# Constants of an attention and mixture-of-experts kernel: from GpSimd's DMA queue to ScalarE's, two of them as rows that TensorE turns into columns

## The chip, the cores and the metric

The kernel runs on one core of a Trainium2 chip. The metric is the device time of one execution in microseconds. Three runs of the kernel before gave 579.92, 584.13 and 584.41 us, a median of 584.13 us.

## The reference: what is computed

Two stages, all in fp32 for the reader of the output:

```python
# q, k, v: [8 batches, 8 heads, 576 tokens, 64]; g_norm: [64]
kv  = einsum('bhsd,bhse->bhde', k, v)          # 64 x 64 for each head
out = einsum('bhsd,bhde->bhse', q, kv)
x   = out / sqrt(mean(out*out, -1) + 1e-6) * g_norm   # -> [4608 tokens, 512]
# mixture of experts, top 1: w_gate [512, 8], w1 [8, 512, 1024], w2 [8, 1024, 512]
logits = x @ w_gate;  e = argmax(logits);  gate = softmax(logits)[e]
# the first `capacity` tokens of each expert are kept, the others give zero
out[i] = gate * relu(x[i] @ w1[e]) @ w2[e]
```

The small inputs are `g_norm` (64 floats), `w_gate` (512 x 8 floats) and `capacity` (one 64-bit integer, here 1152). They are the constants of which the change speaks.

## The kernel before

**Attention** goes through the eight batches in order. A batch's k, v and q come in two halves of four heads each; a half is loaded by two DMAs of SyncE's (SP's) queue (lines 685 and 686: 512 KB in rows of 1 KB, and 64 KB in rows of 256 bytes), in the order k, v, k, v, q, q. Three buffers stand ready for each of k, v and q. TensorE (PE) makes kv of each pair of heads (line 707), ScalarE or VectorE copies it out as `kvs` and into a block-diagonal table `kv_bd`, PE turns `kvs` (line 731) and multiplies it by the gate weights `wgs` (line 740), so that the logits of a token come out of the same product as its row: `kv_bd` has 64 + 8 columns for each head. PE turns q (line 771) and multiplies it by `kv_bd` (line 789). VectorE, ScalarE and GpSimd (POOL) work out the norm, the expert and the place of each token, and POOL writes the rows to a scratch tensor `x_dram` (lines 1006 and 1008).

**Experts** follow one after the other: weights are loaded by SP's queue, split into fp16 high and low parts, the expert's rows are gathered by indirect DMAs, and PE makes both products (lines 522 and 568) from three fp16 terms each. The result is scattered by indirect DMAs (line 598).

**Where the constants are used.** `g_norm` stands as a column `gcol`, one value for each of 128 partitions (the 64 values twice). It scales the gate weights once (line 265, in place) and later the scale of the first expert matrix (lines 347 and 366). `cap` is the capacity as a column and is used when the tables of the tokens that are left over are made, hundreds of us later. `wgs` is first read by PE at line 740, in the first batch.

**What sets the order.** Everything ahead of the planner (memsets, iotas, the loads of the constants, line 265) is put into the engines' streams by the framework's scheduler. From the first load of k on, the class `Plan` lists operations with their engine, estimated duration, key and what they need, places them greedily, and the instructions are then emitted in that order, engine by engine (`manual_schedule`). Each engine runs its stream strictly in order. DMAs of the hardware queues (SP's and ScalarE's) count on eight completion semaphores, taken in turn (`DMAHW0` to `DMAHW7` in the listings below); a DMA whose semaphore is still in use waits on its issuing engine until the earlier DMA on that semaphore has landed. DMAs of POOL's queue have eight of their own (`DMASW0` to `DMASW7`).

Of the kernel before, what the change touches and what calls it, by code (L numbers as in the profile page):

```python
# [11 lines left out]
F32 = mybir.dt.float32  # L12
I32 = mybir.dt.int32
AF = mybir.ActivationFunctionType
ALU = mybir.AluOpType
# [29 lines left out]
FIRST = -50.0  # L45
# [33 lines left out]
class Ring:  # L79
# [3 lines left out]
    def new(self):  # L83
        self.holds.append(Hold(self.holds[-self.n] if len(self.holds) >= self.n else None))
        return self.holds[-1]
# [8 lines left out]
class Plan:  # L94
# [5 lines left out]
    def op(self, ways, fn, deps=(), key=0.0, takes=(), uses=(), late=0.0):  # L100

        ways = [ways] if isinstance(ways[0], str) else list(ways)
        o = Op(ways, fn, [d for d in deps if d is not None], list(takes), key, late)
        for h in takes + uses if isinstance(takes, tuple) and isinstance(uses, tuple) else list(takes) + list(uses):
            h.users.append(o)
        self.ops.append(o)
        return o
# [56 lines left out]
def attention_moe_kernel(  # L164
# [12 lines left out]
    nc = tc.nc  # L177
    NB, H, S, D = q.shape
# [3 lines left out]
    P = 128  # L182
# [10 lines left out]
    cst = ctx.enter_context(tc.tile_pool(name="cst", bufs=1))  # L193
# [10 lines left out]
    ones = cst.tile([1, P], F32, name="ones")  # L204
# [43 lines left out]
    warm = cst.tile([1, 1], F32, name="warm")  # L248
    nc.vector.memset(warm, 0.0)
    nc.scalar.activation(warm, warm, AF.Exp)  # L250
    cap_i = cst.tile([P, 2], I32, name="cap_i")
    nc.gpsimd.dma_start(cap_i, capacity.bitcast(I32).rearrange("(o x) -> o x", o=1).broadcast_to([P, 2]))
    cap = cst.tile([P, 1], F32, name="cap")
    nc.vector.tensor_copy(cap, cap_i[:, 0:1])

    gcol = cst.tile([P, 1], F32, name="gcol")
    for h2 in range(2):
        nc.gpsimd.dma_start(gcol[h2 * D:(h2 + 1) * D], g_norm.rearrange("(d o) -> d o", o=1))

    wgs = cst.tile([P, 2, 2, 2, E], F32, name="wgs")  # L260
    nc.vector.memset(wgs, 0.0)
    for f in range(2):
        for i in range(2):
            nc.gpsimd.dma_start(wgs[i * D:(i + 1) * D, f, i], w_gate.rearrange("(f i g p) e -> f i p g e", f=2, i=2, g=2)[f, i])
    nc.vector.tensor_scalar(out=wgs, in0=wgs, scalar1=gcol, scalar2=None, op0=ALU.mult)


    kv_bds = []
# [377 lines left out]
    tab, misc = bank("tab"), bank("misc")  # L646
# [17 lines left out]
    op = plan.op  # L664
# [5 lines left out]
    def copy(e, out_, in_):  # L670
        if e == "A":
            nc.scalar.copy(out_, in_)  # L672
        else:
            nc.vector.tensor_copy(out_, in_)

    issued, waits = [], []

    def load(b):
        ts = {}
        for j, (nm, half) in enumerate(ORDER):  # L680
            h = new(nm)
            h.t, h.flat = ios[nm, (len(rings[nm].holds) - 1) % NIO]

            def go(e, h=h, src={"k": k, "v": v, "q": q}[nm], hs=slice(half * HH, (half + 1) * HH)):
                nc.sync.dma_start(h.t[:, :, 1:C], src[b, hs, HP:S].rearrange("h (p c) d -> p h c d", c=C - 1))
                nc.sync.dma_start(h.t[0:HP, :, 0], src[b, hs, 0:HP].rearrange("h p d -> p h d"))

            o = op(("S", ISSUE), go, [], (b - 2) * C + j * 0.8, takes=(h,))
            ts[nm, half] = h, op(("D", LOAD), None, [o], takes=(), uses=(h,))
            issued.append(o)  # L690
        return ts

    def kv_products(b, ts):

        key = (b - 1) * C + 1
        kv = new("kv")
        kv2 = kv.t = kv_bds[b % 2]
        a = new("a")
        rows = [slice(0, D), slice(D, P)]

        def product(i):
            def go(e):
                a.t = a.t or bank("a")
                for c in range(C):
                    for g in range(2):
                        h = 2 * (i % 2) + g
                        nc.tensor.matmul(a.t[rows[g], i * D:(i + 1) * D], lhsT=kh.t[:, h, c, :], rhs=vh.t[:, h, c, :],
                                         start=(c == 0), stop=(c == C - 1))

            kh, vh = ts["k", i // 2][0], ts["v", i // 2][0]  # L710
            return op(("T", 1.16), go, [ts["k", i // 2][1], ts["v", i // 2][1]], key, (a,), (kh, vh))

        mm = [product(i) for i in range(HH)]
        ks, kt, a2, a3 = new("kvs"), new("kvt"), new("a"), new("a")

        def apart(e):
            ks.t = at.tile([P, HH * D], F32, name="kvs", bufs=1)
            copy(e, ks.t, a.t[:, 0:HH * D])

        done = [op([("A", 0.29), ("V", 0.34)], apart, mm, key + 1, (ks,), (a,))]  # L720

        def spread(g, f):

            return op([("A", 0.29), ("V", 0.34)],
                      lambda e: copy(e, kv2[rows[f]].rearrange("p (i g) f x -> p i g f x", g=2)[:, :, g, f, 0:D],
                                     ks.t[rows[g]].rearrange("p (i x) -> p i x", i=HH)), done[0:1], key + 1.5, (kv,), (ks,))

        def turn(e):
            a2.t = bank("a")
            for f in range(2):  # L730
                nc.tensor.transpose(a2.t[:, f * P:(f + 1) * P], ks.t[:, f * P:(f + 1) * P], ident)

        def keep(e):
            kt.t = at.tile([P, 2 * P], F32, name="kvt", bufs=1)
            copy(e, kt.t, a2.t[:, 0:2 * P])

        def gates(e):
            a3.t = bank("a")
            for f in range(2):
                nc.tensor.matmul(a3.t[:, f * 4 * E:(f + 1) * 4 * E], lhsT=kt.t[:, f * P:(f + 1) * P],  # L740
                                 rhs=wgs[:, f].rearrange("p i g e -> p (i g e)"), start=True, stop=True)

        o = op(("T", 0.22), turn, done[0:1], key + 1, (a2,), (ks,))
        o = op([("A", 0.29), ("V", 0.34)], keep, [o], key + 1, (kt,), (a2,))
        o = op(("T", 0.2), gates, [o], key + 1, (a3,), (kt,))
        done = [spread(g, f) for g in range(2) for f in range(2)]
        for g in range(2):
            for f in range(2):
                done.append(op([("A", 0.11), ("V", 0.13)],
                               lambda e, g=g, f=f: copy(  # L750
                                   e, kv2[rows[f]].rearrange("p (i g) f x -> p i g f x", g=2)[:, :, g, f, D:XW],
                                   a3.t[rows[g], 0:H * E].rearrange("p (i g x) -> p i g x", g=2, x=E)[:, :, g]),
                               [o] + done[4:], key + 2, (kv,), (a3,)))
        return kv, done
# [493 lines left out]
    def finish():  # L1248
# [8 lines left out]
        early["rank"] = op(("V", 3.4), lambda e: rank_experts(cnt_all), [o, o2], key + 0.1)  # L1257

    tiles = {0: load(0)}
    kvs = {0: kv_products(0, tiles[0])}  # L1260
    for b in range(NB):
        oh, ssh = new("o"), new("ss")
        oh.t, ssh.t = o_sbs[b % NO], sss[b % NO]
        if b + 1 < NB:
            tiles[b + 1] = load(b + 1)
        outs, sums, by_u = [], [], {}
        for n in range(len(UNITS)):
            done = unit(b, n, tiles[b], *kvs[b], oh)
            outs += done
            u = UNITS[n][1]  # L1270
            by_u.setdefault(u, []).extend(done)
            if UNITS[n][0]:
                sums += [squares(b, c, by_u[u], oh, ssh) for c in range(2 * u, min(2 * u + 2, C))]
            if n == 1 and b + 1 < NB:
                kvs[b + 1] = kv_products(b + 1, tiles[b + 1])
        route(b, oh, ssh, outs, sums)
        if b == PICK_AFTER:
            early_weights()
        if b == EARLY_AFTER:
            early_slots()  # L1280
# [210 lines left out]
    op = plan.op  # L1491
# [8 lines left out]
    def weights(r, key, after, after2):  # L1500

        ws, sets, zs, holds = wsets[r % 2], [], [], []
        for i in range(2):
# [9 lines left out]
            for p in range(4):  # L1513
                o = op(("S", 0.7), lambda e, i=i, p=p, regs=regs: load(e, i, p, regs),
                       [regs.get("op"), early["rank"]] + after + (early["free"][p] if r == 1 and i == 0 else [])
                       + (after2 if i else []), key,
                       (raws[p],))
                regs.setdefault("op", o)
                loads.append(op(("D", 1.46), None, [o], key, (), (raws[p],)))
# [115 lines left out]
    o = op(("S", 0.01), moved, [early["scaled"]], -9 * KEY, (), tuple(ews))  # L1635
# [6 lines left out]
    for r in range(E):  # L1642
        products(r, *args)
        key = KEY * r
        if r + 1 < E:
            before = [] if r > 1 else sent
            st, xs_hold, sl, gates, turned, sent, asked = rows_beside(r + 1, key + ROWS)
# [3 lines left out]
        else:  # L1651
            steps, o = plan_rest(), early["later"]
            for _ in range(68):
                o = op(("V", 0.2), lambda e: next(steps, None), [o], key + 1)
# [36 lines left out]
```

## Time and profile before

| what | us |
|---|---|
| runs: lowest, median, highest | 579.92, 584.13, 584.41 |
| the profiled execution | 582.53 |
| its span | 580.7 |
| PE busy | 530.1 (91%) |
| VectorE (DVE) busy | 384.1 (66%) |
| ScalarE (ACT) busy | 256.0 (44%) |
| GpSimd (POOL) busy | 218.2 (38%) |

The span is the time between the first and the last instruction of the program's record; 1.8 us of the profiled execution lie outside it. Busy times are sums over stages with different limits, so the stage that holds the change has to be read by itself. SPq is SP's queue, in which DMAs are issued; the time of such an instruction is the time of its issue, not of the transfer.

### The profile page before, as it was taken

Reading aid. Unit: us, or ns where it says so; the run is one execution under the profiler, and the core shown is the slowest. Engines: PE = TensorE matmul, PEld = TensorE weight load, DVE = VectorE, ACT = ScalarE, POOL = GpSimd, SP = SyncE. Lnnn points to the kernel's source line nnn. Section 1 sums busy time; section 2 is a strip of 40 time slices with the busy share of each in tenths; the row PEclk is TensorE's granted clock in tenths of the full one; section 3 lists DMA queues with packets and bytes.
Section 4 is the critical chain, followed back from the end, with each engine's and each line's share of the span. In section 5 each row is a group of like instructions: output and inputs, shape, how many; then the busy total and the mean of one; then the engine's idle time right before and its main releaser. Section 6 shows DMA issues by size and latency. Waiting matters only on the chain.

```text
span 580.7 us, 11581 instructions
## 1 busy us (share of the span) xinstructions
PE 530.1 (91%) x4339; PEld 354.9 (61%) x4339; DVE 384.1 (66%) x998; ACT 256.0 (44%) x498; POOL 218.2 (38%) x300
## 2 busy tenths in 40 slices
PE   1887999777887999998999999999999999999995
PEld 1886998666543656643765477477558747845442
DVE  2386687989985898999999375738638634731200
ACT  1465675678621356372725252453525355211210
POOL 7002053265315478384342713364163352011011
PEclk9999899999999999999999999999999999999999
DMA  7999999956228759697864653847265342001001
GB/s 208 291 301 332 326 309 345 333 174 247 93 92 306 204 113 358 122 309 206 217 227 118 169 174 98 209 102 240 82 171 181 110 82 68 1 36 40 1 20 48
DMA packets 94302, 102.56 MB, mean 177 GB/s; under 512 B 51314, under 2 KB 75890, under 8 KB 93216
## 3 DMA queue, kind: packets, MB, share of 16 engines
q1 hardware_dynamic: 86240, 70.43, 44.6%
q0 software_dynamic: 8000, 31.32, 15.4%
q8 instruction: 36, 0.59, 0.4%
q14 instruction: 26, 0.21, 0.1%
HBM read 73.13 MB, written 20.61 MB: 161 GB/s over the span
## 4 chain that ended last, share of the span: by engine, by line
PE 28%; issue 19%; DMA 12%; DVE 11%; POOL 6%; ACT 2%; POOLq 0%; DVEq 0%; SPq 0%
PE hp L522 12%; PE yp L568 12%; DMA out_dram<-ysb,si 8%; DVE w2l L377 3%; DMA xg<-x_dram,gi 2%; DVE am L337 2%; POOL xg L433 2%; DVE hl L530 2%; PE yp L577 1%; POOL pair L469 1%; POOL xm L441 1%; PE op L522 1%; DMA raw<-in_moe_w_dram 1%; POOL out_dram L598 1%; DVE w1l L377 1%
## 5 line engine op out<-in xcount | busy, mean ns | idle before, releaser
L522 PE MATMUL hp<-xs,w1h 128*128 128x320 f16 (+6 forms) x896 | 133.5, 300 | 1.8 <-DVE hl L530 1.7
L522 PEld LDWEIGHTS <-w1h 128*128 128x128 f16 x960 | 93.2, 98 | 42.5 <-issue 5.6
L568 PEld LDWEIGHTS <-hh 128*128 128x128 f16 x560 | 54.4, 98 | 64.6 <-issue 1.9
L598 POOL DMA_INDIRECT out_dram<-ysb,si x41 | 42.2, 1030 | 135.3 <-ACT ysb L593 104.1
L527 ACT ACTIVATE hh<-hp 128x320 f16<-128x320 f32 (+7 forms) x64 | 40.7, 636 | 110.5 <-PE hp L522 110.4
L337 DVE TENSOR_REDUCE am<-raw 128x1 f32<-128x512 f32 x120 | 75.4, 674 | 6.5 <-DMA raw<-in_moe_w_dram 6.3
L522 PE MATMUL hp<-xs,w1l 128*128 128x320 f16 (+6 forms) x448 | 71.5, 300 | 0.0
L530 DVE SCALAR_TENSOR_TENSOR hl<-hp,hh 128x320 f16<-128x320 f32 (+7 forms) x64 | 47.2, 737 | 34.0 <-ACT hh L527 33.6
L469 POOL TENSOR_TENSOR pair<-xm,pair 128x512 f16<-128x512 f32 (+5 forms) x35 | 43.0, 1228 | 69.0 <-ACT pair L465 64.1
L568 PE MATMUL yp<-w2h,hl 128*128 128x512 f16 x272 | 66.0, 385 | 0.0
L789 PE MATMUL op<-kv_bd,qt 128*128 128x144 f32 (+1 forms) x384 | 57.9, 293 | 8.1 <-ACT qt L672 3.2
L568 PE MATMUL yp<-w2h,hh 128*128 128x512 f16 x272 | 64.6, 379 | 0.8 <-ACT ysb L593 0.8
L568 PE MATMUL yp<-w2l,hh 128*128 128x512 f16 x272 | 64.5, 379 | 0.0
L593 ACT ACTIVATE ysb<-yp,ysc 128x512 f32<-128x512 f32 (+5 forms) x40 | 27.3, 683 | 81.7 <-PE yp L568 68.7
L377 DVE SCALAR_TENSOR_TENSOR w2l<-raw,sw,w2h 128x512 f16<-128x512 f32 x64 | 53.2, 878 | 9.5 <-ACT w2h L371 9.5
L433 POOL DMA_INDIRECT xg<-x_dram,gi x41 | 42.7, 1040 | 42.1 <-DVE gi L632 29.2
L522 PEld LDWEIGHTS <-w1l 128*128 128x128 f16 x480 | 46.7, 98 | 19.0
L789 PEld LDWEIGHTS op<-kv_bd,qt 128*128 128x128 f32 x384 | 50.1, 195 | 11.8 <-ACT o_sb L672 4.6
L377 DVE SCALAR_TENSOR_TENSOR w1l<-raw,sg,w1h 128x512 f16<-128x512 f32 x64 | 52.3, 868 | 1.7 <-ACT w1h L371 1.7
L568 PEld LDWEIGHTS <-hl 128*128 128x128 f16 x280 | 27.3, 99 | 33.2 <-issue 2.2
L371 ACT ACTIVATE w1h<-raw,sg 128x512 f16<-128x512 f32 x62 | 39.8, 712 | 7.3 <-DVE sg L366 7.2
L371 ACT ACTIVATE w2h<-raw,sw 128x512 f16<-128x512 f32 x62 | 39.7, 710 | 3.0 <-PE yp L577 2.1
(249 smaller groups left out, 651.7 us busy)
## 6 DMA issues: line engine op xcount, KB each, us to landing
raw<-in_moe_w_dram SPq DMA_DIRECT2D x64, 512.0 KB, 5.1
x_dram<-o_sb POOLq DMA_DIRECT2D x8, 1152.0 KB, 8.1
k_sb<-in_k_dram SPq DMA_DIRECT2D x16, 512.0 KB, 7.5
v_sb<-in_v_dram SPq DMA_DIRECT2D x16, 512.0 KB, 7.4
q_sb<-in_q_dram SPq DMA_DIRECT2D x16, 512.0 KB, 8.4
x_dram<-o_sb POOLq DMA_DIRECT2D x8, 144.0 KB, 7.9
k_sb<-in_k_dram SPq DMA_DIRECT2D x16, 64.0 KB, 7.1
v_sb<-in_v_dram SPq DMA_DIRECT2D x16, 64.0 KB, 7.9
```

The costliest lines, as they stand in the source:

```text
L337: nc.vector.tensor_reduce(out=am()[:, p:p + 1], in_=raw[:, sl(p)], axis=AX.X, op=ALU.max, apply_absolute_value=True)
L371: nc.scalar.activation(wh[:, sl(p)], raw[:, sl(p)], AF.Copy, scale=z["s"])
L377: nc.vector.scalar_tensor_tensor(out=wl[:, sl(p)], in0=raw[:, sl(p)], scalar=z["s"], in1=wh[:, sl(p)], op0=ALU.mult, op1=ALU.subtract)
L433: nc.gpsimd.indirect_dma_start(out=self.xg[i][0:n], out_offset=None, in_=x_dram[0:self.rows, :], in_offset=bass.IndirectOffsetOnAxis(ap=se ...
L469: nc.gpsimd.tensor_tensor(out=pair[0:n, 1], in0=self.xm[i][0:n], in1=pair[0:n, 0], op=ALU.subtract)
L522: nc.tensor.matmul(self.view(hp)[:, u], lhsT=w[:, c, j * P:(j + 1) * P], rhs=x[:, c, u * hw:(u + 1) * hw], start=(t == 0 and c == 0), stop ...
L527: nc.scalar.activation(self.out(self.hh, j), self.view(hp), AF.Relu)
L530: nc.vector.scalar_tensor_tensor(out=self.out(self.hl, j), in0=self.view(hp), scalar=0.0, in1=self.out(self.hh, j), op0=ALU.max, op1=ALU.s ...
L568: nc.tensor.matmul(yp[0:n, 0:DM], lhsT=h[:, j, o:o + n], rhs=w[:, j, :], start=(m == 0), stop=(m == len(self.terms) - 1))
L593: nc.scalar.activation(self.ysb[0:n], yp[0:n, 0:DM], AF.Copy, scale=self.ysc[0:n, i:i + 1])
L598: nc.gpsimd.indirect_dma_start(out=out[:, :], out_offset=bass.IndirectOffsetOnAxis(ap=self.sidx[0:n, col:col + 1], axis=0), in_=ysb[0:n], ...
L789: nc.tensor.matmul(ph.t[:, j * m:(j + 1) * m], lhsT=qt.t[:, i * P:(i + 1) * P], rhs=x, start=True, stop=True)
```

## The change

The six small loads leave POOL's queue for ScalarE's. `w_gate` still comes as before, four DMAs of 64 partitions. `g_norm` now comes once, as a row of 64 values in one partition, and `capacity` as two integers in one partition. Three new operations of the plan make columns of them: VectorE doubles the row and casts the capacity (`widen`), PE multiplies the row by a one and the capacity by a row of ones, into two columns of a PSUM bank (`constants`), VectorE copies the two columns out and scales `wgs` (`columns`). PE's product with `wgs` names `columns` as something that it needs. POOL issues no DMA before `x_dram`'s first.

```diff
-    cap_i = cst.tile([P, 2], I32, name="cap_i")
-    nc.gpsimd.dma_start(cap_i, capacity.bitcast(I32).rearrange("(o x) -> o x", o=1).broadcast_to([P, 2]))
+    cap_i = cst.tile([1, 2], I32, name="cap_i")
     cap = cst.tile([P, 1], F32, name="cap")
-    nc.vector.tensor_copy(cap, cap_i[:, 0:1])
+    caprow = cst.tile([1, 1], F32, name="caprow")
 
     gcol = cst.tile([P, 1], F32, name="gcol")
-    for h2 in range(2):
-        nc.gpsimd.dma_start(gcol[h2 * D:(h2 + 1) * D], g_norm.rearrange("(d o) -> d o", o=1))
+    grow = cst.tile([1, 2, D], F32, name="grow")
+    one = cst.tile([1, 1], F32, name="one")
+    nc.vector.memset(one, 1.0)
 
     wgs = cst.tile([P, 2, 2, 2, E], F32, name="wgs")
     nc.vector.memset(wgs, 0.0)
     for f in range(2):
         for i in range(2):
-            nc.gpsimd.dma_start(wgs[i * D:(i + 1) * D, f, i], w_gate.rearrange("(f i g p) e -> f i p g e", f=2, i=2, g=2)[f, i])
-    nc.vector.tensor_scalar(out=wgs, in0=wgs, scalar1=gcol, scalar2=None, op0=ALU.mult)
+            nc.scalar.dma_start(wgs[i * D:(i + 1) * D, f, i], w_gate.rearrange("(f i g p) e -> f i p g e", f=2, i=2, g=2)[f, i])
+    nc.scalar.dma_start(grow[:, 0], g_norm.rearrange("(o d) -> o d", o=1))
+    nc.scalar.dma_start(cap_i, capacity.bitcast(I32).rearrange("(o x) -> o x", o=1))
...
+    def constants(e):
+        nc.tensor.matmul(misc[:, 128:129], lhsT=grow.rearrange("o h d -> o (h d)"), rhs=one, start=True, stop=True)
+        nc.tensor.matmul(misc[:, 129:130], lhsT=ones, rhs=caprow, start=True, stop=True)
+
+    def columns(e):
+        nc.vector.tensor_copy(gcol, misc[:, 128:129])
+        nc.vector.tensor_copy(cap, misc[:, 129:130])
+        nc.vector.tensor_scalar(out=wgs, in0=wgs, scalar1=gcol, scalar2=None, op0=ALU.mult)
+
+    def widen(e):
+        nc.vector.tensor_copy(grow[:, 1], grow[:, 0])
+        nc.vector.tensor_copy(caprow, cap_i[:, 0:1])
+
+    ready = op(("V", 0.2), widen, [], FIRST, late=9.0)
+    ready = op(("V", 0.5), columns, [op(("T", 0.2), constants, [ready], FIRST)], FIRST)
...
-        o = op(("T", 0.2), gates, [o], key + 1, (a3,), (kt,))
+        o = op(("T", 0.2), gates, [o, ready], key + 1, (a3,), (kt,))
```

The order of the streams moves at the start of the program alone. Behind the first twenty-odd instructions of each engine the same instructions follow in the same order.

SP's stream at the start, before (`k_sb_181` and `v_sb_183` are the first half batch, `k_sb_188` and `v_sb_190` the second, `q_sb_185` and `q_sb_192` its queries):

```order
L685 DMA k_sb_181<-in_k_dram 128x4x256
L686 DMA k_sb_181<-in_k_dram 64x4x64
L685 DMA v_sb_183<-in_v_dram 128x4x256
L686 DMA v_sb_183<-in_v_dram 64x4x64
L685 DMA k_sb_188<-in_k_dram 128x4x256
L686 DMA k_sb_188<-in_k_dram 64x4x64
L685 DMA v_sb_190<-in_v_dram 128x4x256
L686 DMA v_sb_190<-in_v_dram 64x4x64
L685 DMA q_sb_185<-in_q_dram 128x4x256 [waits DMAHW0_49]
L686 DMA q_sb_185<-in_q_dram 64x4x64 [waits DMAHW1_49]
```

And now (each buffer's number is one higher, each line's 18):

```order
L703 DMA k_sb_182<-in_k_dram 128x4x256
L704 DMA k_sb_182<-in_k_dram 64x4x64
L703 DMA v_sb_184<-in_v_dram 128x4x256
L704 DMA v_sb_184<-in_v_dram 64x4x64
L703 DMA k_sb_189<-in_k_dram 128x4x256 [waits DMAHW1_49]
L704 DMA k_sb_189<-in_k_dram 64x4x64 [waits DMAHW3_49]
L703 DMA v_sb_191<-in_v_dram 128x4x256 [waits DMAHW4_49]
L704 DMA v_sb_191<-in_v_dram 64x4x64 [waits DMAHW5_49]
L703 DMA q_sb_186<-in_q_dram 128x4x256 [waits DMAHW6_49]
L704 DMA q_sb_186<-in_q_dram 64x4x64 [waits DMAHW7_49]
```

The order of the loads is the same. The first eight went out without a wait, now the first four do: the constants' DMAs have taken places among the eight semaphores. The fifth load (`k_sb_189`) waits for the first, the seventh (`v_sb_191`) for the first DMA of `wgs` (semaphore 4), the eighth for the large load of `v_sb_184` (semaphore 5).

ScalarE's stream now (before, the table load and `warm` were followed at once by the copy of `kvs`):

```order
L265 DMA grow<-in_g_norm_dram 1x64
L266 DMA cap_i<-in_moe_capacity_dram 1x2
L250 ACT_TABLE_LOAD
L250 ACTIVATE warm<-warm 1x1 [waits DVE_49]
L264 DMA wgs<-in_moe_w_gate_dram 64x2x8 [waits DVE_49]
L264 DMA wgs<-in_moe_w_gate_dram 64x2x8
L264 DMA wgs<-in_moe_w_gate_dram 64x2x8 [waits DMAHW0_49]
L264 DMA wgs<-in_moe_w_gate_dram 64x2x8 [waits DMAHW2_49]
L674 COPY kvs<-a 128x256 [waits PE_49]
```

Two of the DMAs stand ahead of the table load, four behind it, and the last two of `wgs` wait until `grow` and `cap_i` have landed.

PE's stream at the start, before and now. Before:

```order
L707 MATMUL a<-v_sb_183,k_sb_181 64x64 [waits DMAHW1_49,DMAHW3_49,DVE_49,Pool_49]
L707 MATMUL a<-v_sb_183,k_sb_181 64x64
L707 MATMUL a<-v_sb_183,k_sb_181 64x64 [waits DMAHW2_49,DMAHW0_49]
L707 MATMUL a<-v_sb_183,k_sb_181 64x64 x17
L707 MATMUL a<-v_sb_190,k_sb_188 64x64 [waits DMAHW5_49,DMAHW7_49,DVE_49,Pool_49]
```

Now:

```order
L725 MATMUL a<-v_sb_184,k_sb_182 64x64 x17
L681 MATMUL misc<-one,grow 128x1 [waits DMAHW0_49,DVE_49]
L682 MATMUL misc<-caprow,ones 128x1 [waits DVE_49]
L725 MATMUL a<-v_sb_191,k_sb_189 64x64 [waits DMAHW5_49,DMAHW3_49,Pool_49]
L725 MATMUL a<-v_sb_191,k_sb_189 64x64
```

The two products that make columns stand between the first half batch's product and the second's, and wait for VectorE's `widen`.

## Rows read from the trace of the kernel before

**Rows 1.** Part 2 of the page: DMA engines' busy tenths in 40 slices of 14.5 us.

```profile
DMA  7999999956228759697864653847265342001001
```

**Rows 2.** Stretches: start:end us, PE, PEld, DVE, ACT, POOL busy, granted clock, DMA share, GB/s.

```profile
2.00:6.00 4.00, 0.00 (x0) 0.00 (x0) 1.06 (x9) 0.20 (x1) 4.00 (x7) 1.00 0.88 242
6.00:8.40 2.40, 0.00 (x0) 0.00 (x0) 0.00 (x0) 0.00 (x0) 2.11 (x9) 1.00 0.50 141
8.40:11.00 2.60, 0.00 (x0) 0.00 (x0) 1.39 (x6) 0.00 (x0) 2.54 (x6) 1.00 0.95 278
15.40:20.00 4.60, 4.51 (x51) 3.84 (x51) 1.53 (x4) 1.55 (x4) 0.00 (x0) 1.00 1.11 291
20.00:54.50 34.50, 31.43 (x433) 29.10 (x433) 22.49 (x70) 22.46 (x56) 3.53 (x11) 1.00 1.12 314
54.50:57.50 3.00, 0.02 (x1) 0.03 (x1) 1.77 (x6) 0.72 (x4) 0.82 (x4) 0.88 1.13 281
57.50:63.80 6.30, 6.30 (x51) 5.84 (x52) 3.82 (x17) 2.64 (x6) 1.15 (x2) 0.52 1.14 287
63.80:110.00 46.20, 43.61 (x530) 39.91 (x530) 37.65 (x117) 33.55 (x84) 15.08 (x42) 1.00 1.09 335
```

**Rows 3.** Timeline of SP's queue: start us, us of the issue, line, transfer.

```profile
0.72 0.46 SPq L685 DMA_DIRECT2D k_sb<-in_k_dram  x1
3.30 0.60 SPq L685 DMA_DIRECT2D k_sb<-in_k_dram  x1
4.60 2.28 SPq L685 DMA_DIRECT2D v_sb<-in_v_dram  x1
6.93 0.61 SPq L686 DMA_DIRECT2D v_sb<-in_v_dram  x1
```

**Rows 4.** Line 686 at 2.6 and 6.9 us: issue ns, start us, us until landing.

```profile
L686 SPq DMA_DIRECT2D v_sb<-in_v_dram x1: 607/607/607, 2.7 to 2.7; - x1
...
DMA to landing us min/median/max: 8.2/8.2/8.2
...
L686 SPq DMA_DIRECT2D v_sb<-in_v_dram x1: 607/607/607, 6.9 to 6.9; - x1
...
DMA to landing us min/median/max: 8.4/8.4/8.4
```

**Rows 5.** Line 685's first load, in the same view.

```profile
DMA to landing us min/median/max: 4.4/4.4/4.4
```

**Rows 6.** Timeline of POOL, and DMA issues of the first 30 us (median us to landing).

```profile
2.15 0.76 POOL L252 DMA_DIRECT2D cap_i<-in_moe_capacity_dram  x1
2.90 1.11 POOL L258 DMA_DIRECT2D gcol<-in_g_norm_dram  x2
8.18 2.36 POOL L264 DMA_DIRECT2D wgs<-in_moe_w_gate_dram  x4
43.21 0.59 POOL L1008 DMA_DIRECT2D x_dram<-o_sb  x1 [32.14 <-DVE kv_bd L674]
...
wgs<-in_moe_w_gate_dram POOLq DMA_DIRECT2D x4, 4.0 KB, 6.2
```

**Rows 7.** Timelines of ACT, DVE and PE; brackets: idle before, and what ended it.

```profile
0.71 1.28 ACT L250 ACT_TABLE_LOAD   x1 [0.71 <-PEq L1673]
17.86 0.37 ACT L672 COPY kvs<-a 128x256 f32<-128x256 f32 x1 [15.50 <-PE a L707]
9.41 0.15 DVE L254 CAST cap<-cap_i 128x1 f32<-128x1 int32 x1 [6.24 <-DMA cap_i<-in_moe_capacity_dram]
11.03 2.40 PE L707 MATMUL a<-v_sb,k_sb 128*64 128x64 f32 x40 [11.03 <-DMA v_sb<-in_v_dram]
15.42 2.40 PE L707 MATMUL a<-v_sb,k_sb 128*64 128x64 f32 x40 [1.99 <-DMA v_sb<-in_v_dram]
19.99 0.65 PE L740 MATMUL a<-wgs,kvt 128*128 128x32 f32 x4
57.50 1.08 PE L771 MATMUL qp<-ident,q_sb 128*128 128x128 f32 x4 [2.98 <-DMA q_sb<-in_q_dram]
```

## The prediction

> **What bounds the kernel now.** The page's part 2 is read first, because the change moves transfers: the DMA engines are at nine tenths or more from the second slice of 14.5 us to the eighth, and at seven in the first [rows 1]. That is the attention stage, which streams q, k and v. The stretches tell more [rows 2]. From 20.0 to 54.5 us the engines move 314 GB/s at a share above 1, and PE is busy 31.4 of 34.5 us: transfers and PE keep the same pace. At 57.5 us PE has still waited 2.98 us for a half of q [rows 7], so up to there the stream of loads sets the time. From 57.5 to 110 us PE is busy 49.9 of 52.5 us and the loads no longer limit. Whatever the change does to the stream before 20 us therefore moves everything behind it by about as much, and nothing else in the program is touched: the streams of all engines are the same behind the start. The question is how many microseconds the load stream gains or loses in its first 20.
>
> Two things are to be seen in that start. **First, the stream runs dry.** It moves 242 GB/s from 2.0 to 6.0 us, 141 GB/s to 8.4 us, and 278 after that [rows 2]. By 8.4 us that is 4.0 x 0.242 + 2.4 x 0.141 = 1.31 MB; at the 0.29 MB/us of 15.4 to 20.0 us it is 4.5 us of work, done in 6.4: 1.9 us are lost. SP is not waiting for a landing then: its seventh load is issued at 4.60 us, takes 2.28 us to issue where its neighbours take 0.6, and the eighth leaves at 6.93 [rows 3]. **Second, a load lands late.** The small half of the first v is issued at 2.65 us (2.7 in its row) and lands 8.2 us later, at 10.85 [rows 4]; PE's first product starts at 11.03 [rows 7]. By 10.85 us 1.31 + 2.45 x 0.278 = 1.99 MB had moved, though the first four loads are 1.18 MB: 0.81 MB, or 2.8 us, had overtaken it. For the very first load, issued at 0.72 and landed 4.4 us later at 5.1 [rows 3, 5], the same sum gives 3.1 x 0.242 - 0.52 = 0.23 MB, 0.8 us. So about 2.0 us of lateness come on top: a few of the sixteen DMA engines must lag, and a load is complete when its slowest engine is.
>
> **The change, part by part.**
>
> *POOL loses seven DMA issues*, 0.76 + 1.11 + 2.36 = 4.23 us [rows 6]. Its memsets end that much earlier, near 7 us. POOL then stands idle until 43.2 us, 32.1 us of idle time [rows 6], and PE's first product waits for v longer than for any memset, so this is worth 0.
>
> *ScalarE gains six issues.* At SP's 0.46 to 0.61 us [rows 3, 4] that is about 3.5 us. Two stand ahead of the table load and push it by some 1.2 us. ScalarE has nothing to do between the table load and 17.86 us, 15.5 us of idle time [rows 7]: 0, unless its copy of `kvs` came before 7 us.
>
> *VectorE and PE gain the columns.* Five small VectorE operations at the 0.15 us of the cast of `cap` are 0.75 us; the scaling of `wgs` only moves forward. Between 15.4 and 20.0 us VectorE is busy 1.53 of 4.60 us, and before that it stood idle 6.24 us for `cap` alone [rows 2, 7]: 0. The two products of one column cost PE at most 2 x 0.16 us (0.65 us for four of line 740) in a place where it waits 1.99 us for the second v: 0 [rows 7]. They add a wait, though: all of PE's stream, the second half batch's product first, now stands behind `grow` and `cap_i`. POOL's constants needed 6.2 us [rows 6]; issued by 2 us they would land by 8.2, before PE reaches them at 11.0 + 2.4 us, or at 8 + 2.4 if loads come sooner. That cover holds by 2 us in the worse case.
>
> *Four loads instead of eight go out at once.* The semaphores that the constants take make the fifth load wait for the first: issued at 5.1 us in place of 3.30. From the first issue to the first bytes pass some 1.4 us (0.72 to a little after 2). The first four loads, 1.18 MB, keep the engines busy from 2.0 to 6.1 us, the fifth's bytes come at 6.5: 0.4 us lost. The seventh load, issued at 4.60 us before, now waits for the first DMA of `wgs`. That one leaves ScalarE at 0.71 + 2 x 0.6 + 1.28 + 0.2 = 3.4 us. How soon a small transfer of ScalarE's queue lands no row shows. From below, the first k took 4.4 us, of which 512 KB at 0.29 are 1.8: 2.6 us, so 6.0 us. From above, the same transfers by POOL took 6.2 us: 9.6 us. The fifth and sixth loads feed the engines from 6.5 to 8.5 us, so the seventh must be issued by 7.1. At 6.0 nothing is lost, at 9.6 it is 2.5 us. I take a landing at 7.4, nearer to the hardware queue's row since it is that kind of queue, and 0.3 us lost. Together the stream loses 0.7 us instead of 1.9: **-1.2 us**, between -1.5 and +1.0 (0.4 + 2.5 against 1.9).
>
> *The late engines.* Between 4 and 10 us POOL's small transfers share the engines with the loads: `cap_i`, whose 1 KB is issued at 2.15 us, keeps VectorE waiting until 9.41, 7.3 us later [rows 6, 7]. Whether these transfers make the engines lag, or merely suffer with them, the trace does not say. The gain is between 0 and the 2.0 us above; I take half, **-1.0 us**. [...]
>
> **Sum:** 582.53 - 1.2 - 1.0 = 580.3 us for a profiled execution. The median of the runs shown lies 1.6 us above the profiled one; I add half of that and forecast 581.1 us.
>
> **Rivals.**
>
> *No change.* Only issue time is saved, on an engine that nobody waits for, and the dry stretch and the late engines belong to the first transfers of a program, whoever issues the constants. For it: the seventh load's issue already hangs at 4.60 us, well before POOL's first transfer lands [rows 3, 7]. Against it: the stream recovers at 8.4 us, about when that transfer lands (9.4). Then the loss of 0.4 us eats what is left: 582 to 584 us. [...]
>
> *Slower: a wait on a semaphore takes the place of the early issue.* If the late engines stay late, the seventh load waits for `wgs` until 9.6 us and the eighth for the large load of the first v, which lands near 10 us. The eighth was issued at 6.93 us and landed at 15.33 [rows 4]; issued at 8.4 to 10.2 us with the same 8.4 us it lands 1.5 to 3.3 us later, and PE's second product, the queries behind it and the rest follow. That gives 584 to 586 us. It decides at 7.1 us: a later landing of the first DMA of `wgs` starves the engines. For it: POOL's 6.2 us; against it: a DMA that comes late finds a short queue.
>
> *A larger gain.* While PE waits for q before 57.5 us its granted clock falls, and from 57.5 to 63.8 us it is 0.52, close to the lower of its two levels, with PE busy all 6.30 us [rows 2]. If an earlier stream shortens that wait enough that the clock stays, half of the 6.3 us come back: 580.3 - 3.1 = 577.2 us. Against it: stream and PE start earlier together, so the wait moves and stays.
>
> **How the numbers follow.** Forecast 0.48 (579.0 to 582.7), no change 0.25 (582 to 584.5), slower 0.17 (584 to 586), larger gain 0.10 (576.5 to 579.5). The range from 577.5 to 586.0 leaves out part of the last case and a tail of the slow one; the runs shown differ by 4.5 us by themselves. One per cent, 5.8 us about the median of 584.13, is what a measurement of this kernel tells from no change: below 578.3 lie most of the larger gain and a small part of the forecast, 0.12; above 590 only a slow start together with a second fall of the clock, 0.03; the rest, 0.85, is within.
>
> **What would show it.** In the changed profile: the first product of PE well before 11 us, the second before 15.4; more than 141 GB/s between 6.0 and 8.4 us; the fifth load issued near 5.1 and the seventh near 7.4 us; the constants' products on PE without idle time that a constant ends; the wait for q before 57.5 us ended earlier by the same amount. A second product of PE at 16 us or later would make the prediction wrong, as would an unmoved start, or an end that has not moved with it.

## The result, and the profile after

The changed kernel is slower, by six parts in a thousand: a median of 587.29 us (581.62 to 589.23 in 22 runs) against 583.42 us (579.92 to 587.28 in 22 runs) for the kernel before, a ratio of 1.0062 with a 95% interval of 1.0044 to 1.0081. The forecast was 581.1 us and the range ended at 586.0. Both the direction and the range were wrong. Here and below a ratio leaves out executions over 1.5% longer than the fastest of their kernel, and medians and ranges keep them, so that a ratio need not be the quotient of two medians. The profiled execution took 587.23 us, its span 585.4 us, 4.7 us more than the 580.7 us of before.

The start went as forecast, or better. Timeline of SP's queue in the changed kernel, answering [rows 3], with four later loads: start, us of the issue, line, transfer.

```profile
0.72 0.46 SPq L703 DMA_DIRECT2D k_sb<-in_k_dram  x1
5.02 0.37 SPq L703 DMA_DIRECT2D k_sb<-in_k_dram  x1
7.16 0.37 SPq L703 DMA_DIRECT2D v_sb<-in_v_dram  x1
7.57 0.61 SPq L704 DMA_DIRECT2D v_sb<-in_v_dram  x1
...
14.52 0.57 SPq L703 DMA_DIRECT2D k_sb<-in_k_dram  x1
37.24 0.81 SPq L703 DMA_DIRECT2D q_sb<-in_q_dram  x1
53.10 0.55 SPq L703 DMA_DIRECT2D q_sb<-in_q_dram  x1
114.80 0.73 SPq L703 DMA_DIRECT2D q_sb<-in_q_dram  x1
```

The fifth load leaves at 5.02 us (5.1 forecast), the seventh at 7.16 (7.4 forecast). The last four rows are set against the same four loads of the kernel before, in the same view:

```profile
17.47 0.55 SPq L685 DMA_DIRECT2D k_sb<-in_k_dram  x1
37.13 0.68 SPq L685 DMA_DIRECT2D q_sb<-in_q_dram  x1
51.19 0.83 SPq L685 DMA_DIRECT2D q_sb<-in_q_dram  x1
110.04 0.64 SPq L685 DMA_DIRECT2D q_sb<-in_q_dram  x1
```

Subtract row by row: the changed kernel is 2.95 us ahead at the first of them, 0.11 behind at the second, 1.91 behind at the third, 4.76 behind at the last. A lead of 3 us is gone by 37 us, and 4.8 us more are lost by 115, all in the attention stage. Behind it nothing is added: the spans differ by 4.7 us as well.

The stretches show the pace (start:end us, PE, PEld, DVE, ACT and POOL busy, granted clock, DMA share, GB/s; they answer [rows 2]):

```profile
2.00:6.00 4.00, 0.00 (x0) 0.00 (x0) 3.08 (x16) 1.02 (x2) 3.76 (x10) 1.00 0.88 268
6.00:8.40 2.40, 0.40 (x8) 0.43 (x10) 0.40 (x2) 0.00 (x0) 0.78 (x4) 1.00 0.96 270
8.40:11.00 2.60, 2.60 (x42) 2.48 (x38) 0.00 (x0) 0.00 (x0) 0.00 (x0) 1.00 0.99 269
15.40:20.00 4.60, 4.19 (x34) 3.74 (x33) 1.81 (x6) 3.34 (x9) 0.00 (x0) 1.00 1.14 273
20.00:54.50 34.50, 29.53 (x407) 27.29 (x405) 21.89 (x68) 19.98 (x50) 3.35 (x10) 0.95 1.13 289
54.50:57.50 3.00, 0.63 (x4) 0.52 (x4) 1.41 (x4) 1.16 (x6) 1.17 (x5) 1.00 1.11 250
57.50:63.80 6.30, 3.92 (x39) 3.50 (x40) 2.77 (x17) 0.82 (x2) 0.32 (x1) 0.52 1.14 266
63.80:110.00 46.20, 41.89 (x510) 38.49 (x509) 34.78 (x103) 31.14 (x76) 15.81 (x44) 0.99 1.09 324
```

Up to 8.4 us the stream is better: 270 GB/s in place of the 141 of the dry stretch. From 15.4 us on every stretch is worse: 273 against 291, 289 against 314, 250 against 281, 266 against 287, 324 against 335. The DMA share is the same as before, 1.13 against 1.12 in the long stretch. So the engines are not waiting for work; the same busy time moves 8% less. In the page's tenths (part 2, against [rows 1]) little of this is seen: the first slice is fuller (8 against 7), and so are the ninth and tenth, where loads that are late still run (6 and 7 against 5 and 6).

```profile
DMA  8999999967326778878882743747276333001001
```

What ScalarE, VectorE and PE do (timelines of these engines, answering [rows 7]; brackets: idle before, and what ended it):

```profile
0.72 0.53 ACTq L265 DMA_DIRECT2D grow<-in_g_norm_dram  x1
1.53 1.28 ACT L250 ACT_TABLE_LOAD   x1 [1.53 <-PEq L1691]
2.25 0.69 ACTq L264 DMA_DIRECT2D wgs<-in_moe_w_gate_dram  x1
14.88 0.37 ACT L674 COPY kvs<-a 128x256 f32<-128x256 f32 x1 [11.85 <-PE a L725]
...
4.93 0.14 DVE L691 CAST caprow<-cap_i 1x1 f32<-1x1 int32 x1 [0.69 <-DMA cap_i<-in_moe_capacity_dram]
...
8.00 2.40 PE L725 MATMUL a<-v_sb,k_sb 128*64 128x64 f32 x40 [8.00 <-DMA v_sb<-in_v_dram]
10.33 0.58 PE L681 MATMUL misc<-one,grow 1*128 1x1 f32 x2
10.78 0.56 PE L682 MATMUL misc<-caprow,ones 1*128 1x1 f32 x2
12.44 2.40 PE L725 MATMUL a<-v_sb,k_sb 128*64 128x64 f32 x40 [1.10 <-DMA v_sb<-in_v_dram]
26.27 1.82 PE L725 MATMUL a<-v_sb,k_sb 128*64 128x64 f32 x40 [2.68 <-DMA v_sb<-in_v_dram]
59.88 1.08 PE L789 MATMUL qp<-ident,q_sb 128*128 128x128 f32 x4 [4.26 <-DMA q_sb<-in_q_dram]
73.56 0.63 PE L789 MATMUL qp<-ident,q_sb 128*128 128x128 f32 x4 [1.30 <-DMA q_sb<-in_q_dram]
105.35 1.06 PE L789 MATMUL qp<-ident,q_sb 128*128 128x128 f32 x8 [1.48 <-DMA q_sb<-in_q_dram]
```

PE's first product starts at 8.00 us in place of 11.03, the second at 12.44 in place of 15.42: 3.0 us gained twice. The two products that make columns (10.33 and 10.78) show no idle time that a constant ends. Then the waits for loads grow: the wait for q that ended at 57.50 after 2.98 us now ends at 59.88 after 4.26, and two more appear. PE's waits from 57 to 112 us, first of the kernel before, then of the changed one (us in total, times, longest), say the same:

```profile
PE qp L771 <- DMA q_sb<-in_q_dram: 3.0, 1, 3.0
```

```profile
PE qp L789 <- DMA q_sb<-in_q_dram: 7.0, 3, 4.3
```

The view of the DMA queues from 15 to 40 us gives the price of a packet. Total of the window, then SP's queue with its packets, MB and share of the 16 engines' time, before:

```profile
DMA packets 10076, 7.43 MB, mean 297 GB/s; under 512 B 3672, under 2 KB 10073, under 8 KB 10073
...
q1 hardware_dynamic: 10069, 7.39, 111.6%
```

and after:

```profile
DMA packets 9086, 6.78 MB, mean 271 GB/s; under 512 B 3214, under 2 KB 9083, under 8 KB 9083
...
q1 hardware_dynamic: 9083, 6.74, 112.8%
```

The mix is the same (36% and 35% of the packets are under 512 B), the share is the same, the count is not: 1.116 x 16 x 25 us / 10069 = 44.3 ns for a packet before, 1.128 x 16 x 25 / 9083 = 49.7 ns after. A share above 100% says that the times of packets overlap, so this is the time from a packet's recorded start to its end, and not what one engine spends on it alone. **The question for the experiments was why the same transfer costs 12% more** in a stretch in which the changed kernel loads no constant any more.

One thing the order of the streams does not show is where the tiles lie. The diff puts three new tiles, `caprow`, `grow` and `one`, into the pool `cst`, and every tile that is allocated behind them moves up by 576 bytes of each partition. The addresses in the two built programs: `k_sb` number 0, the first of the nine buffers of k, v and q, starts at byte 105632 before and at 106208 after. All nine are 5376 bytes apart, 21 x 256, so they share one offset: 160 bytes past a multiple of 256 before, 224 past it after. Within a buffer each row of a load, of 1 KB or of 256 bytes, starts at a multiple of 256 from the buffer's start.

### The profile page after: what moved, and what is told of

Its sections match the earlier page's. It is cut to its first block, busy times and chain, and to the rows that moved or that the text cites. A ratio compares the mean times of both kernels' runs of the same rounds, so it can differ in the third digit from the quotient of the medians.

```text
span 585.4 us, 11587 instructions
## 1 busy us (share of the span) xinstructions
PE 532.1 (91%) x4343; PEld 356.3 (61%) x4343; DVE 386.4 (66%) x1002; ACT 256.3 (44%) x498; POOL 215.2 (37%) x293
## 3 DMA queue, kind: packets, MB, share of 16 engines
q1 hardware_dynamic: 86240, 70.43, 46.2%
## 4 chain that ended last, share of the span: by engine, by line
PE 28%; DVE 19%; issue 16%; DMA 8%; POOL 3%; ACT 3%; POOLq 0%; DVEq 0%
PE hp L524 13%; PE yp L570 12%; DMA out_dram<-ysb,si 6%; DVE w2l L379 5%; DVE am L339 4%; DVE w1l L379 4%; DMA xg<-x_dram,gi 2%; DVE hl L532 2%; PE yp L579 1%; PE op L524 1%; ACT w2h L373 1%; POOL xg L435 1%; POOL out_dram L600 1%; DVE xm L443 0%; ACT sq L831 0%
## 5 line engine op out<-in xcount | busy, mean ns | idle before, releaser
L570 PE MATMUL yp<-w2h,hl 128*128 128x512 f16 x272 | 66.3, 387 | 0.0
```

The costliest lines, as they stand in the source:

```text
L570: nc.tensor.matmul(yp[0:n, 0:DM], lhsT=h[:, j, o:o + n], rhs=w[:, j, :], start=(m == 0), stop=(m == len(self.terms) - 1))
```

## The experiments

Two theories stood at first. **Addresses**: the shifted buffers make every load slower. **Skew**: POOL's late constants had held the first half batches apart, and without them the loads collide with each other. The first four kernels separate them, and the queue from the form of the constants. They were timed on one chip, beside 35 runs of the kernel before with a median of 584.38 us.

**The kernel before, shifted.** 576 bytes that nobody uses, and nothing else:

```diff
+    pad = cst.tile([P, 144], F32, name="pad")
+    nc.vector.memset(pad[0:1, 0:1], 0.0)
     wgs = cst.tile([P, 2, 2, 2, E], F32, name="wgs")
```

> The kernel before with 576 bytes of padding for each partition ahead of wgs, so that every tile behind it (the buffers of q, k, v among them) lies where the changed kernel has it; queues and order as before. Theory of the addresses (the load stream of the changed kernel is slower because its buffers moved): from 15 to 40 us a packet of SP's queue takes about 50 ns instead of 44, and without the gain of 3 us at the start the time is 4 to 7 us over before, 587 to 590 us. Theory of the skew (POOL's small transfers left a few DMA engines some 2 us behind the others, and a stream whose engines are out of step is faster): nothing moves, 44 ns and 583.4 us. Theory of the queue (ScalarE's transfers or their semaphores leave the stream slower): 583.4 us.

Measured: 588.97 us, ratio 1.0087 (1.0053 to 1.0120). SP's queue from 15 to 40 us:

```profile
q1 hardware_dynamic: 9102, 6.70, 112.6%
```

That is 1.126 x 400 / 9102 = 49.5 ns for a packet, the price of the changed kernel, in a program that has none of its operations. The shift alone makes the kernel slower.

**The changed kernel with POOL's transfers put back**, into a tile that is not yet in use (`raw1`, created earlier). They are seven DMAs (one of `capacity`, two of `g_norm`, four of `w_gate`) where ScalarE's queue now has six:

```diff
+    nc.gpsimd.dma_start(raw1[:, 0:2], capacity.bitcast(F32).rearrange("(o x) -> o x", o=1).broadcast_to([P, 2]))
+    for h2 in range(2):
+        nc.gpsimd.dma_start(raw1[h2 * D:(h2 + 1) * D, 2:3], g_norm.rearrange("(d o) -> d o", o=1))
...
+            nc.gpsimd.dma_start(raw1[i * D:(i + 1) * D, 8:72].rearrange("p (f i g e) -> p f i g e", f=2, i=2, g=2)[:, f, i], w_gate.rearrange("(f i g p) e -> f i p g e", f=2, i=2, g=2)[f, i])
```

> The changed kernel with POOL's seven transfers of before put back beside the new ones, into a region that is not read before the first expert's weights overwrite it. Addresses and ScalarE's queue as in the changed kernel. Skew: some engines lag again by about 2 us, packets take 44 ns, the first product of PE starts near 11 us and the time goes back to 582 to 584 us. Addresses: packets stay at 50 ns, the start is late again, 588 to 591 us. Queue: packets stay at 50 ns, 587 us or more.

Measured: 588.23 us, ratio 1.0049 (1.0016 to 1.0082). Its profiled execution took 594.71 us, the longest of the twelve, so only its first microseconds are read. PE's first product:

```profile
9.69 2.40 PE L729 MATMUL a<-v_sb,k_sb 128*64 128x64 f32 x40 [9.69 <-DMA v_sb<-in_v_dram]
```

With POOL's transfers back, the late start is partly back (9.69 against 8.00 us), and the time stays long. The skew theory, which asked for 582 to 584 us here, falls. The kernel before, shifted, speaks against it as well, with POOL's transfers and 49.5 ns, and so does the queue alone further down, without them and at 45.3 ns.

**The changed kernel at the old addresses.** The three new tiles become pieces of `raw1`:

```diff
+    raw1 = wts.tile([P, KD * F], F32, name="raw1")
-    caprow = cst.tile([1, 1], F32, name="caprow")
+    caprow = raw1[0:1, 129:130]
-    grow = cst.tile([1, 2, D], F32, name="grow")
-    one = cst.tile([1, 1], F32, name="one")
+    grow = raw1[0:1, 0:128].rearrange("o (h d) -> o h d", h=2)
+    one = raw1[0:1, 128:129]
```

> The changed kernel with its three new small tiles put into a region that is free at the start, so that all buffers of q, k, v lie where they lay before. Queues and order as in the changed kernel. Addresses: PE starts at 8 us, packets take 44 ns, and the 3 us of the start stay: 580 to 581 us. Skew and queue: 50 ns, 587 us as the changed kernel.

Measured: 581.33 us (579.47 to 585.22), ratio 0.9955 (0.9922 to 0.9987). SP's queue from 15 to 40 us, and PE's first product:

```profile
q1 hardware_dynamic: 9730, 7.16, 108.1%
```

```profile
8.01 2.40 PE L725 MATMUL a<-v_sb,k_sb 128*64 128x64 f32 x40 [8.01 <-DMA v_sb<-in_v_dram]
```

Packets at 44.4 ns as before, the start at 8.01 as in the changed kernel. The edit without its side effect makes the kernel 0.45% faster, 2.6 us, with an interval from 0.8 to 4.6 us. Its trace, of an execution of 583.87 us, does not show a lead of 3 us carried to the end. Three of the loads that were compared above:

```profile
15.02 0.67 SPq L703 DMA_DIRECT2D k_sb<-in_k_dram  x1
36.62 0.72 SPq L703 DMA_DIRECT2D q_sb<-in_q_dram  x1
109.08 0.71 SPq L703 DMA_DIRECT2D q_sb<-in_q_dram  x1
```

Against before this is 2.45 us ahead, then 0.51, then 0.96. Against the changed kernel, which differs only in where its tiles lie, it is 0.50 us behind, then 0.62 ahead, then 5.72 ahead. So the address costs the changed kernel some 6 us of the attention stage, and most of the early lead goes without it, in a wait of PE for v. First before, then this kernel:

```profile
27.12 1.39 PE L707 MATMUL a<-v_sb,k_sb 128*64 128x64 f32 x40 [0.64 <-DMA v_sb<-in_v_dram]
```

```profile
26.75 2.40 PE L725 MATMUL a<-v_sb,k_sb 128*64 128x64 f32 x40 [2.70 <-DMA v_sb<-in_v_dram]
```

The changed kernel has the same wait, 2.68 us until 26.27, and in both the granted clock from 20.0 to 54.5 us is 0.95 where it was 1.00 before. The bytes moved from 0 to 37 us, before and in this kernel, say that the stream itself was less far ahead than PE:

```profile
DMA packets 13114, 9.63 MB, mean 260 GB/s; under 512 B 4764, under 2 KB 13112, under 8 KB 13112
```

```profile
DMA packets 13711, 9.84 MB, mean 266 GB/s; under 512 B 5172, under 2 KB 13709, under 8 KB 13709
```

The difference of 0.21 MB is 0.7 us at 0.29 MB/us. The gain of 0.45% is the runs', not that trace's.

**The queue alone.** The kernel before with its seven column transfers issued by ScalarE, at the old addresses (the first of them; `gcol` and `wgs` likewise):

```diff
-    nc.gpsimd.dma_start(cap_i, capacity.bitcast(I32).rearrange("(o x) -> o x", o=1).broadcast_to([P, 2]))
+    nc.scalar.dma_start(cap_i, capacity.bitcast(I32).rearrange("(o x) -> o x", o=1).broadcast_to([P, 2]))
```

> One part of the change alone: the kernel before, constants as columns, but the seven transfers issued by ScalarE instead of POOL. Addresses as before. Addresses: packets 44 ns, start as early as in the changed kernel (8 to 9 us), 580 to 582 us. Skew: no POOL transfers, engines in step, 50 ns, 586 to 588 us. Queue: 586 to 588 us as well.

Measured: 583.19 us, ratio 0.9985 (0.9950 to 1.0021), no difference. Packets take 45.3 ns, the first product starts at 9.27 us. By these traces the queue gives part of the earlier start (11.03 to 9.27), and the rows in place of columns, with what comes with them, the rest (to 8.01). Each is one trace, and the kernel before, shifted, which starts with the same instructions as before, has its first product at 10.21 us; so the parts are rough. At the end the queue by itself gives nothing that these runs can tell from zero.

**Which addresses, and where do they bend.** The next four kernels start from the one at the old addresses and move only the buffers: a `head` in front of the nine, and a `tail` behind them, 512 bytes together, so that all else keeps its place within 256. They ran on another chip, beside 7 runs of the kernel before with a median of 584.31 us.

```diff
+    head = io.tile([P, 16], F32, name="head")
+    nc.vector.memset(head[0:1, 0:1], 0.0)
...
+    tail = io.tile([P, 112], F32, name="tail")
+    nc.vector.memset(tail[0:1, 0:1], 0.0)
```

With 64 bytes in front the buffers have the changed kernel's offset, 224:

> Kernel e3 (changed kernel, buffers where they were before) with the nine buffers of q, k and v alone moved by 64 bytes, so that they begin at 224 bytes beyond a multiple of 256, as in the changed kernel, instead of 160; all tiles ahead of them unmoved, those behind moved by 512. If the place of these buffers within 256 bytes sets the speed of the stream: about 50 ns for a packet from 15 to 40 us and 587 us. If it is another tile's place, or the distance of 576 bytes as such: 44 ns and 581 us.

Measured: 588.27 us, ratio 1.0063 (1.0039 to 1.0087), packets 49.0 ns. The nine buffers are enough to bring the whole loss.

With 96 in front they start on a multiple of 256:

> Kernel e3 with the nine buffers moved by 96 bytes, so that each begins at a multiple of 256 bytes; the tiles behind moved by 512. [...] If only certain places are bad (224) and others equal: 44 ns and 581 us.

Measured: 576.73 us (575.98 to 577.43), ratio 0.9869 (0.9845 to 0.9893): faster than both kernels. SP's queue from 15 to 40 us, three stretches, and the only wait for q that is left up to 64 us:

```profile
DMA packets 11602, 8.57 MB, mean 343 GB/s; under 512 B 4230, under 2 KB 11597, under 8 KB 11597
...
q1 hardware_dynamic: 11597, 8.51, 109.1%
```

```profile
20.00:54.50 34.50, 29.75 (x442) 27.44 (x441) 24.58 (x82) 21.74 (x56) 4.56 (x14) 0.99 1.09 345
54.50:57.50 3.00, 3.00 (x17) 2.99 (x16) 2.08 (x8) 1.66 (x4) 1.16 (x2) 0.56 1.13 335
57.50:63.80 6.30, 6.30 (x85) 5.92 (x84) 4.76 (x8) 3.88 (x10) 0.00 (x0) 1.00 1.06 381
```

```profile
50.39 0.63 PE L793 MATMUL qp<-ident,q_sb 128*128 128x128 f32 x4 [0.32 <-DMA q_sb<-in_q_dram]
```

A packet takes 37.6 ns and the stream runs at 343 GB/s where before it ran at 297. PE waits 0.32 us for q in place of 2.98. The clock from 57.5 to 63.8 us is granted in full where it was 0.52 [rows 2]; it is low earlier instead, 0.56 from 54.5 to 57.5 us where it was 0.88. Packets at 37.6 ns are also cheaper than those of the changed kernel's start (41.3 ns from 8.4 to 11.0 us, by the same sum).

The converse, the other tiles moved by 64 bytes and the buffers left at 160, in one run:

> The counterpart of e5: kv_bd, the tables and the weights' tiles moved by 64 bytes, the buffers of q, k and v and all tiles behind them by 512, that is, unmoved within 512 bytes. Buffers' place: 44 ns, as e3. Another tile's place: 50 ns.

Measured: 580.81 us, packets 46.5 ns. Nothing of the loss in time is there, as far as one run tells; the packets lie between the 44.4 ns of the old addresses and the 49.0 of the moved buffers. And the buffers at 192, in one run:

> Kernel e3 with the nine buffers moved by 32 bytes: they begin at 192 beyond a multiple of 256, a multiple of 64 and not of 256. If 64 bytes are the grain that matters: as fast as e6. If it is 256: between e3 and e5, 44 to 50 ns.

Measured: 584.08 us, packets 44.7 ns.

**Alignment by itself.** Three kernels on a third chip, on which the kernel before had a median of 588.19 us (582.83 to 592.74 in 13 runs). First the kernel before with its buffers on a multiple of 256 (96 bytes in front, 416 behind):

> The kernel before, constants by POOL as columns, with the nine buffers of q, k and v moved by 96 bytes to multiples of 256, the tiles behind them by 512. It tells what the change itself is worth once no buffer stands in a bad place. If place and queue add up: packets of about 38 ns as in e6, a start near 10 us instead of 7 to 8, and e6's 576.7 us plus the 2 to 3 us that POOL's transfers cost at the start, 578.5 to 580 us. If the fast stream makes the start's loss good (the loads are no longer what limits): 576 to 577.5 us, as e6.

Measured: four runs, 582.46, 585.52, 576.75 and 585.42 us. They lie too far apart for a ratio. Packets take 41.5 ns at 319 GB/s; the trace is 5.0 us ahead of that of before up to 212 us, and then loses 4.0 us in one place, in PE's waits from 203 to 236 us:

```profile
PE yp L588 <- issue: 4.0, 1, 4.0
```

The profile names nothing that this wait waits for. It is no matter of alignment: both other traces of this chip have it at the same product, one of them with its buffers at 128 (the next kernel; its line follows), and none of the other ten traces has it.

```profile
PE yp L590 <- DVE bmax L363: 4.7, 1, 4.7
```

The kernel before has no trace on this chip; its median is some 4 us above its medians elsewhere (583.42 to 584.38), which the same wait would explain, though no trace shows it. That the alignment helps the kernel before at the end too is not shown, though its four runs have a median of 583.94 us; that it speeds up its loads is.

The offset 128, in one run:

> Kernel e3 with the nine buffers moved by 224 bytes: they begin at 128 beyond a multiple of 256. If 256 is the grain: 44 ns or more, 581 us or more. If 128 is enough: 38 ns and 577 us.

Measured: 587.57 us beside a median of 588.19 us of before on this chip, packets 46.2 ns.

Last the changed kernel just as it is, with 32 bytes in front of the buffers, from 224 to 256:

```diff
+    head = io.tile([P, 8], F32, name="head")
+    nc.vector.memset(head[0:1, 0:1], 0.0)
```

> The changed kernel as it stands, its new tiles where the change put them, with 32 bytes of padding ahead of the nine buffers: they go from 224 beyond a multiple of 256 to a multiple of 256, the tiles behind move by 32. Place of the buffers: 38 ns, 576 to 578 us, as e6. If e6 was fast for another reason (the tiles behind, the constants' place): 50 ns and 587 us.

Measured: 580.49 us (578.29 to 583.79), ratio 0.9893 (0.9856 to 0.9929); packets 39.6 ns at 332 GB/s. Two lines turn the changed kernel's loss of 0.6% into a gain of 1.1%. Its profiled execution has the same unexplained wait of 4.0 us, until 214.88 us.

All offsets together, each packet time worked out from the same row of the queues' view, 15 to 40 us (the execution of 594.71 us, 51.9 ns at 224, is left out):

| offset past a multiple of 256 | ns per packet | kernels |
|---|---|---|
| 0 | 37.6, 39.6, 41.5 | changed at the old places +96, changed +32, before +96 |
| 128 | 46.2 | changed at the old places +224 |
| 160 | 44.3, 44.4, 45.3, 46.5 | before, changed at the old places, queue alone, others moved |
| 192 | 44.7 | changed at the old places +32 |
| 224 | 49.0, 49.5, 49.7 | changed at the old places +64, before shifted, changed |

These are means over rows of two sizes and a few records of 4 bytes (405 of 10069 before, 357 of 9083 in the changed kernel). Sorted by size, the packet records of the same executions and the same 25 us show which pays: a packet of 1 KB takes 49.3 to 54.7 ns on average at offset 0, 59.3 to 62.2 at 128, 160 and 192, and 66.3 to 66.6 at 224. A packet of 256 bytes takes 18.2 to 20.4 ns on average, with a median of 18 at every offset.

So the measured price has two steps. For 1 KB the offsets 128, 160 and 192 are alike, 4.6 to 12.9 ns above a multiple of 256, and 224 lies another 4.1 to 7.3 ns above them. For 256 bytes no price is seen. No run shows what happens to a packet on its way, so the cause of the steps, and why 224 is so much dearer, is open.

## Why the prediction was wrong

**The dry stretch: right.** The forecast was -1.2 us. By 8.4 us the changed kernel has moved 4.0 x 0.268 + 2.4 x 0.270 = 1.72 MB against 1.31, which at 0.29 MB/us is 1.4 us. The two waits on semaphores came where they were put: the fifth load left at 5.02 us, the first having landed at 5.00, and the seventh at 7.16, the first DMA of `wgs` having landed at 7.14. That DMA was issued at 2.25 us (3.4 forecast), though the table load ahead of it in ScalarE's stream ran until 2.81, and took 4.9 us to land.

**The late engines: the sign right, the size too small at the start, the mechanism not shown.** The forecast took half of 2.0 us. The first and the second product come 3.0 us earlier; 1.4 of it is the fuller stream, so about 1.6 is left for lateness. The traces have sixteen landing records for each of these loads, and a load counts as landed with the last. Before, thirteen of the sixteen of the small half of the first v lie between 7.48 and 8.54 us, and the other three at 8.98, 9.93 and 10.90, just ahead of PE's first product at 11.03; in the changed kernel all sixteen lie between 7.07 and 7.86, with the product at 8.00. The kernel with POOL's transfers put back starts at 9.69, in between, so in that trace these transfers carry 1.7 of the 3.0 us in one way or the other. But a load that lands earlier moves PE and by itself adds no bytes to the stream, and by the prediction's own reading the stream sets the time. The prediction gives no reason why this term should reach the end. What was measured is the lateness that goes with POOL's transfers; no run names an engine or shows what made the last records late.

**The terms set at nothing: right.** POOL's 4.23 us, ScalarE's issues (its copy of `kvs` starts at 14.88 us after 11.85 us of idle time), VectorE's five operations and PE's two products cost nothing on the path. PE's two took 0.58 and 0.56 us in the trace, under the wait for the second v.

**The step that failed** is the one that carries all of these to the end: "Whatever the change does to the stream before 20 us therefore moves everything behind it by about as much, and nothing else in the program is touched: the streams of all engines are the same behind the start." The streams are the same in what they do and in which order; they are not the same in where they write. With the buffers 576 bytes further on, a packet costs 49.7 ns instead of 44.3, and the loads set the time for longer: the prediction read them as no longer limiting behind 57.5 us, and the changed kernel waits for q again at 73.56 and 105.35. The shift alone costs 0.87% (the kernel before, shifted), the nine buffers alone bring it (1.0063 against before with them moved to 224, where 0.9955 was measured at the old place), and the edit alone gains 0.45% (the changed kernel at the old addresses).

The step fails a second time, in the lead itself. In the changed kernel it was 3.0 us at 14.5 us and gone by 37 us; at the old addresses it was 2.45 us at 15 and 0.51 at 37, so most of that loss is not the address. What came early to PE was not all in the stream, and a wait of 2.7 us for v before 27 us took it back. The forecast, 581.1 us, lies next to the 581.33 that the edit without the shift measured, and this is in part luck: it had 2.2 us of gain and 0.8 us added for the level of the runs, the measured gain is anything from 0.8 to 4.6 us, and the one trace has 0.5 to 1 us left of the lead.

The terms of the start were mostly read well. What was missing was a look at the allocation: the diff adds three tiles to a pool that lies ahead of the load buffers, and the effect could have been seen as a question, though not priced, before any run.

**The rivals.** "No change" named the right sum for the queue alone: 0.9985 with the columns moved as they were. "Slower by a semaphore" had the right sign and the wrong mechanism. Its point of decision was 7.1 us, the seventh load left at 7.16, and the engines were not starved: 270 GB/s at that moment. Its times of 584 to 586 us are near what came, by accident. "A larger gain" asked for an earlier stream that keeps the clock up; the aligned kernel is one, with the clock at 1.00 from 57.5 to 63.8 us and at 0.56 in the 3 us ahead of it (before: 0.88 there, and then 0.52 for 6.3 us), so the low stretch is shorter and not gone. Its 576.73 us lie where that rival was put, for another reason: the loads themselves became cheaper.

Still open are the price of 224 against 160, what in POOL's seven transfers makes the first loads land late, how much of the early start arrives at the end, and the wait of 4.0 to 4.7 us near 216 us in the three traces of the third chip.

## What to carry to other kernels

When an edit adds, drops or resizes a tile, compare the addresses of the DMA destinations behind it in the pools, besides the order of the instructions: this kernel, whose loads set the pace of its attention stage, changed by 1.1% through 64 bytes (0.9955 of before with its buffers at 160, 1.0063 at 224). Try the buffers that are streamed into on multiples of 256 bytes within the partition, the cheapest place here (37.6 to 41.5 ns for a packet against 44.3 to 49.7 elsewhere), and keep them there with a pad that is part of the code. If two traces have the same DMA share and different GB/s, divide share by packets first (here 44.3 and 49.7 ns at 111.6% and 112.8%): a dearer packet is not a wait, and looking for a wait finds only its consequences.

## What the runs showed of the hardware that was not expected

- The time of a load's packets went with the SBUF address that it writes to. From 15 to 40 us the mean was 37.6 to 41.5 ns when they start on a multiple of 256 bytes, 44.3 to 46.5 at 128, 160 and 192 past it, and 49.0 to 49.7 at 224; the packets of 1 KB paid it, and those of 256 bytes had a median of 18 ns at every offset. In the changed kernel with only its buffers moved the stream of one core went from 272 GB/s (224) over 288 (160) to 343 (0).
- The first large loads landed later where POOL's small transfers ran beside them: in the traces with POOL's seven constants in flight PE's first product starts at 9.69 to 11.03 us at the offsets 160 and 224, each time behind a load, and at 8.89 at offset 0, behind VectorE; with the changed kernel's rows on ScalarE's queue alone it starts at 7.74 to 8.45 us, and at 7.09 and 7.14 at offset 0.
- The DMA share of a window is no measure of what is moved: 1.13 went with 289 GB/s, 1.12 with 314 and 1.09 with 345, in the same 34.5 us.
